# Exponentials among gelus and attention tiles over a batch's products: a re-planned gated-attention and spatial-gating kernel

## The chip, the cores and the metric

The kernel runs on one core of a Trainium2 chip. A core has five engines, each with its own instruction queue that is worked off in the order written: PE (matrix products), DVE and ACT (element-wise work, ACT also the functions that need a table: exp, log, gelu), POOL (element-wise work on data in on-chip memory) and SP, which here only issues DMA transfers. An instruction waits at the head of its queue until what it reads is there and what it overwrites has been read; everything behind it waits too. The metric is the device time of one execution in microseconds (us), as the median of several runs.

## The reference, cut

```python
# attention part: B, H, S, D = 4, 8, 768, 48
f = 1.0 / (1.0 + np.exp(-f_logit))
state = zeros((B, H, D, D))
for t in range(S):
    state = f[:, :, t, :, None] * state + einsum('bhd,bhe->bhde', k[:, :, t], v[:, :, t])
    y[:, :, t] = einsum('bhd,bhde->bhe', q[:, :, t], state)
x = y.transpose(0, 2, 1, 3).reshape(B, S, H * D)          # (4, 768, 384)

# gated MLP part: d_model 384, d_ff 1024
h = gelu_tanh(x @ w_in)
u, v = h[..., :512], h[..., 512:]
v_n = (v - mean(v)) / sqrt(var(v) + 1e-06) * g_ln          # over the 512 features
v_s = einsum('ts,bsd->btd', w_sg, v_n) + b_sg[None, :, None]
out = x + (u * v_s) @ w_out
```

The recurrence over time is a sum over earlier tokens with decaying weights, so the kernel computes it in chunks with matrix products.

## The kernel before

**Tiles.** Each of the 4 batches has 768 tokens, that is 6 tiles of 128, so 24 tiles, numbered n = 0 to 23. A tile's work is cut into *steps* with short names. The names are used below, so here they are, in the order in which a tile passes through them.

- Loads on SP: `f`, `k`, `q`, `v`.
- Gates: `e` and `l` (ACT: exp, then log, of the gate's logits), `lh`, `ll` (split into a high and a low part), `cum` (PE: cumulative sum), `up`, `dn` (ACT: exp of plus and of minus the sum), `mq`, `mk` (q and k times them).
- Turning q and k so that features lie on partitions. Tiles 0 to 5: `tr` (PE transposes) and `tc` (copies out). Tiles 6 to 23: `tt` (DVE transposes blocks of 32), `to` (DMA to the scratch tensor `kq_d`), `ti` (four DMAs back into the one tile `raw`), `tc` (two copies from `raw` into one of two `sk` tiles, on ACT or DVE). `ti` of tile n needs `tc` of tile n-1 to be done, since there is one `raw`.
- Attention: `su` (PE: 64 small products, scores and state updates, into `ps_s`), `ms` (DVE: mask), `sa`, `sm` (state), `y` (PE: 64 small products into `ps_y`), `ty`, `jy` (ACT copies, DVE adds the two halves of `ps_y`: the tile's x).
- MLP: `xT` (PE transposes x), `xh`, `xl` (ACT, DVE: high and low part), `hv` (PE: 9 products, 512 columns), `gv` (ACT: gelu), `ns`, `nd`, `nq`, `nr`, `nh`, `nl` (normalisation; `nd`, `nq`, `nh` on ACT). Per 3 tiles: `hu` (4 of 9 products) and `gu` (ACT: gelu). Per batch, once all six tiles are normalised: `sg` (8 of 18 products: the spatial product), `sb`, `sm_`, `sh`, `sl` (bias, gate, split), `po` (6 of 12 products), `re` (add x), `out` (store).
- Weights, once: `ld`, `wa` to `wf` (split into high and low parts on ACT, DVE, POOL) and `wT`, `wh`, `wl` (transposed `w_sg`).

**PSUM.** Four banks `ps_b` are shared by `cum`, `tr`, `xT`, `wT`, `hv`, `hu`, `sg` and `po`. A bank is held from the product to the last step that reads it: `hv` to its `gv`, `hu` to its `gu`, `cum` to its `dn`, `sg` to its `sb`, `po` to its `re`, `xT` to its `xl`. PE can't start a product while all four are held.

**What sets the order.** The class `Plan` decides, when the program is written, on which engine each step goes and in which order each engine's queue is written: a list scheduler with durations (`T`, and `W` for DMAs), due times, and a table `MOVES` that shifts due times and fixes engines for some steps. Nothing is decided on the chip. Due times come from a list `order` in which `merge` strews the next batch's attention steps between the products of the present batch, from share `A0` to share `A1` of them. Two costs matter here: `TABLE`, the time of a load of ACT's function table (exp and log are in one table, "E", gelu in another, "G"), and `HOLD`, which is added to the due time of an ACT step that would need the other table. On top of that, two lists of needs named `turn` forbid mixing: `e` of a batch needs the last `gu` and `gv` of the batch before, and each `gv` and `gu` of a batch needs all six `dn` of that batch. So each batch has one phase of exponentials and one of gelus.

**Fillers.** In the first 45 us of the plan, `warm` puts products of zeros (L1047) into stretches in which the plan has PE idle.

Of the kernel before, what the change touches and what calls it, by code (L numbers as in the profile page):

```python
# [63 lines left out]


MOVES = """
wfin0:-0.3:POOL wcin1:48.7 wdin1:106.3:DVE wein1:-89.2 wbin2:27.5 wqin2:32.3 wrin2:71.4 wdin2:34.7 wfin2:57.5:DVE
wbin3:31 wdin3:-0.5:POOL ldin4:0.2 wdin4:2.9:DVE ldin5:-428.9 ldin6:21.4 wdin6:0:DVE wfin6:30.8 wfin7:-35.2
ldout0:74.2 wfout0:0.5 ldout1:50.9 wcout1:144.3 ldout3:147 wrout3:87 wcout3:17.5 wfout3:22.1 wh1.0:-37.6 wT2.1:209.9
ldsg4:160.3 ldsg5:25.7 wh5.0:-25.3 wl5.0:1.4 v0:2.3 tc0.0:-149.1:DVE tc0.1:-170.6:ACT sa0.0:144.7 xh0:5.9 ns0:116.7  # L70
f1:-812.5 k1:-926.4 v1:3.6 mq1:-5:POOL do1:-14.2 tc1.1:-36.6:ACT sm1.1:-14.2:DVE hv1:545.1 v2:439.4 w2.0:-49.3:DVE
sm2.1:-68.3:DVE sg0.0:586.1 sh0.0:-74.9 sm_0.3:0:DVE mq3:7.6 mk3:-107.3 di3:-24.8 sm3.0:53.6:DVE sm3.1:0:POOL nq3:-6.3
nl3:-0.8 f4:28.7 q4:232.9 mq4:-143.4:POOL do4:158.4 di4:225.7:DVE su4:-20.1 sm4.0:26.5:POOL w5.0:344.2 w5.1:-181.4
mk5:-12.7:POOL di5:0.3:ACT gv5:17.2 sm_1.0:23 sl1.0:2.8 sm_1.1:56.2:DVE gu1.2:-28.9 hu1.3:30.8 sg1.3:701.8 sl1.3:-133
w6.0:0:POOL lh6:0:ACT ll6:-2.1 mq6:116.2:DVE tc6.1:112.2:ACT sm6.1:-39.6:DVE re6:-66.3 w7.0:330.6 ll7:-0.7:POOL
up7:73.8 mq7:199.7:DVE mk7:0:POOL sm7.0:25.9:POOL w8.0:-55.9 w8.1:104:POOL e8:24.5 lh8:-0.2 cum8:19.4 tc8.0:-24.4:DVE
su8:-8.5 sm8.0:0:POOL sa8.1:-29 xT8:80.9 sg2.0:205.7 sm_2.2:-53.8:POOL sm_2.3:0:DVE w9.1:-120.3 e9:241.9 ll9:0:POOL
mq9:0:POOL mk9:0:DVE tc9.0:-117:ACT y9:95.9 po9:929.6 w10.1:-30.3:DVE lh10:-23.6 ll10:19.8 ti10.3:0.9 tc10.0:263.6:ACT
w11.0:51.4:POOL lh11:5.2:ACT ll11:5.3:POOL mq11:-39:POOL tt11.0:-9.6 su11:-201.2 nr11:-106.6 sg3.0:1365 sg3.1:1534.6
sm_3.2:137.5 sg3.3:-186.9 re11:-108.1 mq12:0.3 mk12:-0.2:POOL lh13:-75.7 ll13:74.5 sm13.0:-110.3 nh13:-5.9  # L80
ll14:151.9:POOL tc14.0:-18.5:ACT su14:-305 sm_4.3:50.1 re14:8.3 ll15:190.5:DVE tc15.1:63.6:DVE sm15.1:129.3:DVE
xT15:-16.2 w16.0:-121.6 lh16:-156.5:ACT mk16:25.9:POOL tc16.1:162:DVE su16:-606.4 sm16.0:100.7 w17.1:0:POOL l17:-51.2
lh17:-306.2 mk17:-62.1:POOL sa17.0:12 sm17.0:1.6:DVE y17:-275.2 xT17:-1 hv17:-1.3 sg5.0:1216.7 sm_5.1:17.1:POOL
po17:1030.5 mk18:0:POOL tt18.0:28.5 ti18.0:83.3 ti18.3:185.4 tc18.1:69.4:DVE sz18:-10.6 w19.1:51.8:POOL e19:-85.2
ll19:-84.7:DVE ti19.2:-0.1 tc19.1:1.5 su19:-56.9 lh20:35.6 ll20:-89.1:DVE mq20:-3:DVE to20.0:-11.4 su20:-151.9
sb6.0:-93.1 sm_6.0:12.8 gu6.1:100.6 hu6.3:39.5 sg6.3:323.4 q21:6.2 lh21:10.2:ACT mk21:19.7:POOL q22:5.2 w22.1:144:POOL
ll22:-123.3:POOL mk22:-59.2:DVE to22.0:-0.5 tc22.0:16.9:ACT sm22.0:-160.4:POOL w23.0:114.5 w23.1:30.7:DVE
ll23:-67.8:POOL mk23:-30.6 di23.0:1.2 tc23.1:21.8:ACT sm23.0:135.1:DVE sm_7.0:35.3 sm_7.1:-62.3:DVE po23:-7.1
"""


# [1072 lines left out]
```

## Time and profile before

| | |
|---|---|
| median of 3 runs | 391.78 us (389.3 to 392.39) |
| the profiled execution's own time | 390.13 us |
| its span, first to last instruction | 388.3 us |
| mean granted TensorE clock | 0.983 |
| instructions | 11340 |
| DMA | 46.29 MB, mean 119 GB/s |

The span is 1.83 us shorter than the time of the same execution. In the profile, busy times are of one engine; "idle before" is the time an engine stood at the head of its queue before an instruction, and the name behind "<-" is the work that it waited for last. PEclk is the share of full speed that the matrix engine's clock was granted. The stages are read off by windows in us from the start of the span: the first products of `sg` begin at 80, the last batch's run to the end from 345. Rows of the written order, further down, carry the line numbers of the kernel that they belong to: behind the table `MOVES` the changed kernel's lines are three lower.

### The profile page before, as it was taken

The numbers are of one execution on the slowest core, as the hardware profiler recorded it, in microseconds if no ns is written. First come the engines' busy times: TensorE is split into PE (matmuls) and PEld (weight loads), VectorE is DVE, ScalarE is ACT, GpSimd is POOL, SyncE is SP. The second block draws the span as 40 slices with busy tenths as digits, with TensorE's granted clock in tenths as the row PEclk, the third lists the DMA queues.
The fourth block names the chain that finished last, engine by engine and source line by source line (L and its number), as shares of the span: only waits on it lengthen the run. The fifth ranks groups of instructions, "written<-read, shape, count | busy, mean of one in ns | idle before, by whom it ended". The sixth has DMA issues, their size and how long they took to land.

```text
span 388.3 us, 11340 instructions
## 1 busy us (share of the span) xinstructions
PE 364.0 (94%) x4672; PEld 330.1 (85%) x4672; DVE 247.7 (64%) x582; ACT 213.3 (55%) x482; POOL 53.5 (14%) x98
## 2 busy tenths in 40 slices
PE   8999999999997978999998799999989799999994
PEld 3677888899995958899988689999978698899994
DVE  5899889859857754339868654238748845335531
ACT  6576589894651546795462374847444475641100
POOL 2101422202121210104001111100212011100000
PEclk9999999999999999999999899999989899999998
DMA  9999995303668798102788984100577840000012
GB/s 177 228 244 192 216 257 139 100 2 95 152 141 190 170 202 144 22 0 64 186 190 187 190 172 83 22 20 23 125 195 185 171 126 3 22 1 2 1 47 81
DMA packets 145997, 46.29 MB, mean 119 GB/s; under 512 B 117524, under 2 KB 144532, under 8 KB 145940
## 3 DMA queue, kind: packets, MB, share of 16 engines
q1 hardware_dynamic: 145940, 45.51, 52.8%
q8 instruction: 38, 0.62, 0.7%
q14 instruction: 19, 0.16, 0.1%
HBM read 33.64 MB, written 11.85 MB: 117 GB/s over the span
## 4 chain that ended last, share of the span: by engine, by line
PE 48%; DMA 14%; DVE 13%; ACT 11%; SPq 6%; issue 6%; POOL 1%; ACTq 0%; DVEq 0%; POOLq 0%
PE ps_b L694 38%; DMA raw<-kq_d 8%; SPq L602 5%; PE ps_y L670 4%; ACT sk L328 3%; DMA kq_d<-f 2%; PE ps_s L622 2%; DVE kq L541 1%; PE ps_b L699 1%; ACT f L323 1%; DMA kq<-in_k_dram 1%; DMA vs<-in_v_dram 1%; ACT vg L323 1%; DVE st L632 1%; ACT vg L736 1%
## 5 line engine op out<-in xcount | busy, mean ns | idle before, releaser
L694 PE MATMUL ps_b<-w_sg_hi,vh 128*128 128x384 f32 x192 | 65.9, 343 | 0.0
L694 PE MATMUL ps_b<-w_sg_lo,vh 128*128 128x384 f32 x192 | 65.4, 341 | 0.0
L694 PE MATMUL ps_b<-w_sg_hi,vh_lo 128*128 128x384 f32 x192 | 65.4, 341 | 0.0
L694 PE MATMUL ps_b<-w_out_hi,gg 128*128 128x384 f32 x174 | 50.4, 354 | 0.0
L328 ACT COPY sk<-raw 112x512 f32<-112x512 f32 x32 | 18.8, 619 | 33.9 <-DMA raw<-kq_d 33.3
L694 PEld LDWEIGHTS ps_b<-w_sg_hi,vh 128*128 128x128 f32 x192 | 36.6, 191 | 0.1
L694 PEld LDWEIGHTS ps_b<-w_sg_lo,vh 128*128 128x128 f32 x192 | 36.6, 190 | 0.0
L694 PEld LDWEIGHTS ps_b<-w_sg_hi,vh_lo 128*128 128x128 f32 x192 | 36.5, 190 | 0.0
L781 DVE SCALAR_TENSOR_TENSOR tmp<-ps_b,cols,b_bc 128x384 f32<-128x384 f32 x32 | 19.5, 610 | 26.1 <-PE ps_b L694 26.0
L694 PEld LDWEIGHTS ps_b<-w_out_hi,gg 128*128 128x128 f32 x174 | 33.7, 199 | 0.3
L797 ACT CAST gg<-tmp 128x384 fp32r<-128x384 f32 x29 | 14.8, 512 | 34.6 <-DVE tmp L786 33.0
L622 PE MATMUL ps_s<-sk 48*64 48x64 f32 x768 | 23.8, 229 | 9.9 <-ACT sk L328 6.4
L622 PEld LDWEIGHTS ps_s<-sk 48*64 48x64 f32 x768 | 20.6, 133 | 13.5 <-ACT sk L328 10.2
L754 DVE SCALAR_TENSOR_TENSOR vh_lo<-vg,vg_rs,vh 128x512 fp32r<-128x512 f32 x24 | 18.0, 750 | 20.3 <-ACT vh L749 20.2
L694 PE MATMUL ps_b<-w_out_lo,gg 128*128 128x384 f32 x87 | 30.4, 349 | 0.0
L694 PE MATMUL ps_b<-xTh,w_in_hi 128*128 128x384 f32 x84 | 29.1, 346 | 0.0
L670 PEld LDWEIGHTS ps_y<-vs,st 64*64 64x64 f32 x768 | 24.7, 134 | 4.8 <-issue 3.2
L694 PE MATMUL ps_b<-xTh,w_in_lo 128*128 128x384 f32 x84 | 28.3, 337 | 0.3 <-issue 0.3
L694 PE MATMUL ps_b<-xTl,w_in_hi 128*128 128x384 f32 x84 | 28.4, 338 | 0.0
L323 ACT ACTIVATE f<-f 128x384 f32<-128x384 f32 x48 | 24.4, 520 | 6.8 <-DMA f<-in_f_logit_dram 6.3
L670 PE MATMUL ps_y<-vs,st 64*64 64x48 f32 x768 | 27.5, 220 | 0.3 <-ACT u L323 0.3
L694 PE MATMUL ps_b<-w_in_hi,xTl 128*128 128x512 f32 x63 | 25.1, 399 | 2.7 <-DVE xTl L719 2.7
(131 smaller groups left out, 874.3 us busy)
## 6 DMA issues: line engine op xcount, KB each, us to landing
f<-in_f_logit_dram SPq DMA_DIRECT2D x24, 192.0 KB, 3.7
kq<-in_k_dram SPq DMA_DIRECT2D x24, 192.0 KB, 3.7
kq<-in_q_dram SPq DMA_DIRECT2D x24, 192.0 KB, 4.4
vs<-in_v_dram SPq DMA_DIRECT2D x24, 192.0 KB, 3.2
raw<-kq_d SPq DMA_DIRECT2D x36, 128.0 KB, 2.6
out_dram<-tmp SPq DMA_DIRECT2D x24, 192.0 KB, 2.8
kq_d<-tmp SPq DMA_DIRECT2D x18, 192.0 KB, 2.3
kq_d<-f SPq DMA_DIRECT2D x18, 192.0 KB, 3.0
```

Of the source, the lines that this page charges most:

```text
L323: nc.scalar.activation(dst, src, func, **kw)
L328: (nc.scalar.copy if e == "ACT" else ENG[e].tensor_copy)(dst, src)
L541: ENG[e].tensor_mul(kt, kt, f_raw[n])
L602: ENG[e].dma_start(raw[row : row + r1 - r0].rearrange("d b a t -> d b (a t)"), kq_d[n, :, r0:r1, m].rearrange("b r j y -> r b (j y)"))
L622: nc.tensor.matmul(ps_s[rows(score_rows(c, 2 * p + par)), par, p * C : (p + 1) * C], sk[r, 0, p, c], sk[r, 1, p, c], start=True, stop=True)
L632: nc.vector.tensor_mul(sts[0], ps_s[:, :, 0 : NP * C].rearrange("s x (p t) -> s x p t", t=C), mask[:, None, None, :].to_broadcast((P, 2, N ...
L670: nc.tensor.matmul(ps_y[rows(c), half, h * D : (h + 1) * D], a, m, start=start, stop=stop)
L694: nc.tensor.matmul(ps, a, m, start=(j == 0), stop=(j == len(seq) - 1))
L699: nc.tensor.transpose(ps[:, j], x_sb[n][:, j * P : (j + 1) * P], ident)
L754: nc.vector.scalar_tensor_tensor(vl, v_raw.pop(n), rs, vh.bitcast(F32), op0=ALU.mult, op1=ALU.subtract)
L781: nc.vector.scalar_tensor_tensor(t, psum[f"sg{g}.{ft}"][:, :E], g_col[:, ft : ft + 1], b_bc[:, tokens(g)], op0=ALU.mult, op1=ALU.add)
L797: nc.scalar.copy(gt[(g, ft)][0], g_raw[(g, ft)])
```

## The change

It has four parts, none of which alters what is computed.

1. The two `turn` lists are emptied, so exponentials may stand among gelus, with a table load wherever the table changes. `HOLD` goes from 8 to 20.
2. `A0` and `A1` get a value for each batch; the attention tiles of the second batch are strewn over 0.25 to 0.85 of the first batch's products, those of the third and fourth over 0.05 to 0.75.
3. Some planned durations are changed: `tt` 0.65 to 0.48, the copies `tr_c` out of `raw` 0.467 to 0.49 on ACT and 0.6 to 0.46 on DVE, and the DMAs `to`, `ti` and `tj` (the short pieces) longer.
4. `MOVES` is another table, for the new plan.

```diff
-A0, A1 = 0.1, 0.8
+A0, A1 = (0.25, 0.05, 0.05), (0.85, 0.75, 0.75)
...
-    ok_e="DVE:0.25", ... tt="DVE:0.65", zr="POOL:2.2", tr_c="ACT:0.467 DVE:0.6", ...
+    ok_e="DVE:0.25", ... tt="DVE:0.48", zr="POOL:2.2", tr_c="ACT:0.49 DVE:0.46", ...
...
-W = dict(... to=(0.5, 0.65), ti=(0.4, 0.4), tj=(0.35, 0.25), out=(0.45, 0.58))
+W = dict(... to=(0.54, 0.9), ti=(0.43, 0.62), tj=(0.4, 0.45), out=(0.45, 0.58))
...
 MOVES = """
-wfin0:-0.3:POOL wcin1:48.7 wdin1:106.3:DVE wein1:-89.2 wbin2:27.5 wqin2:32.3 wrin2:71.4 wdin2:34.7 wfin2:57.5:DVE
...
+wbin0:388.1 wdin0:-42.7:POOL wcin1:371.6 wrin3:343.8 wcin3:-99.1 wdin3:305.4:DVE wdin4:86.5 wfin4:224.6:DVE wrin5:88.5
...
-    STAY, HOLD, SHIFT, AWAY = 194.7373, 8.0, 31.7708, 4.5365
+    STAY, HOLD, SHIFT, AWAY = 194.7373, 20, 31.7708, 4.5365
...
-            order += merge(units + rest, att, A0, A1)
+            order += merge(units + rest, att, A0[b - 1], A1[b - 1])
...
-        turn = [f"gu{2 * b - 1}.{NF - 1}", f"gv{n0 - 1}"] if (n0 := b * NT) else []
+        turn = [f"gu{2 * b - 1}.{NF - 1}", f"gv{n0 - 1}"] if (n0 := b * NT) < 0 else []
...
-        turn = [f"dn{n0 + j}" for j in range(NT)] if b else []
+        turn = []
         op(f"gv{n}", lambda e, n=n: gelu_v(n), T["gv"], [f"hv{n}"] + turn, table="G", take=("vg",), unbank=f"hv{n}")
```

**ACT, at the second batch's first gelus.** Before, the copies of an attention tile out of `raw` (L328) are followed by the only table load of this batch's gelu phase, and then gelus (`vg`) and normalisation alone:

```order
L797 CAST gg<-tmp 128x384
L328 COPY sk_97<-raw 112x512 x2
L321 ACT_TABLE_LOAD
L323 ACTIVATE vg,vg_mv<-ps_b_68 128x512
L736 ACTIVATE vg<-vg,vg_mv 128x512
L741 ACTIVATE vh_lo,vg_mv<-vg 128x512
```

Now, at the first gelus of the same batch (L320 is the line of table functions, `eb` and `f<-ps_b` are the exponentials `up` and `dn`):

```order
L320 ACTIVATE f,flag_e<-f 128x384
L320 ACTIVATE f<-f 128x384
L318 ACT_TABLE_LOAD
L320 ACTIVATE vg,vg_mv<-ps_b_70 128x512
L794 CAST gg<-tmp 128x384
L325 COPY sk_97<-raw 112x512 x2
L733 ACTIVATE vg<-vg,vg_mv 128x512
L318 ACT_TABLE_LOAD
L320 ACTIVATE eb_103<-ps_b_68 128x8x48
L794 CAST gg<-tmp 128x384
L320 ACTIVATE f<-ps_b_68 128x384
```

Between one gelu and the next a load, the exponentials of later tiles and a second load have moved in. In the whole program, without the branch for inputs out of range, there were 7 table loads after the first one and there are now 35.

**PE, at the third batch's first attention tile (tile 12).** Before, `su` of tile 12 (L622, L627) follows a spatial product of the batch before:

```order
L694 MATMUL ps_b_69<-w_sg_hi_80,vh 128x384
L694 MATMUL ps_b_69<-w_sg_lo_82,vh 128x384
L694 MATMUL ps_b_69<-w_sg_hi_80,vh_lo 128x384
L622 MATMUL ps_s<-sk_96 64x64 x4
L627 MATMUL ps_s<-vs_93,kq_90 48x48 x4
```

Now it follows `y` of tile 11 (L667), the last attention tile of the second batch, directly:

```order
L667 MATMUL ps_y<-S_101,sk_97 64x48 x2
L667 MATMUL ps_y<-vs_95,st 64x48
L667 MATMUL ps_y<-S_101,sk_97 64x48
L619 MATMUL ps_s<-sk_96 64x64 x4
L624 MATMUL ps_s<-vs_93,kq_90 48x48 x4
```

The third batch's attention has moved ahead of the second batch's spatial products; `su` of tiles 12 to 15 and `y` of tiles 12 to 14 now stand before or among the first of these, the rest after them. From `cum14` on, PE's steps there are now, by name: cum14, su11, y10, cum15, xT10, y11, su12, hv9. ACT's over the same stretch, from the last gelu ahead of it: a table load, up14, xh9, ty10, dn14, up15, dn15, xh10, and the two copies `tc` of tile 12. A little later PE has su14, hv12, sg2.0, cum16, y14, su15, and ACT, after the first copy of tile 14: xh12, gu3.2, nh11, ty13, a table load, e16, e18, l16, l18, lh16, e19, a table load, gv12, and the second copy of tile 15.

**PE, at the start.** Before, up to the first `su` (L524 is `cum`, L561 `do`, which picks the decays out, L576 `tr`):

```order
L1047 MATMUL ps_b_67<-zeros 128x512 x3
L524 MATMUL ps_b_67<-f,cs 128x384
L524 MATMUL ps_b_68<-f,cs 128x384
L1047 MATMUL ps_b_69<-zeros 128x512
L1047 MATMUL ps_b_67<-zeros 128x256
L561 MATMUL ps_b_69<-cs,eb_103 112x2 x4
L1047 MATMUL ps_b_67<-zeros 128x128
L576 MATMUL ps_b_70<-cs,kq_90 112x128 x4
L576 MATMUL ps_b_67<-cs,kq_90 112x128 x4
```

Now:

```order
L1044 MATMUL ps_b_67<-zeros 128x512 x2
L521 MATMUL ps_b_67<-f,cs 128x384
L1044 MATMUL ps_b_68<-zeros 128x512
L1044 MATMUL ps_b_68<-zeros 128x128
L521 MATMUL ps_b_68<-f,cs 128x384
L558 MATMUL ps_b_69<-cs,eb_102 112x2 x4
L573 MATMUL ps_b_70<-cs,kq_90 112x128 x4
L573 MATMUL ps_b_67<-cs,kq_90 112x128 x4
```

Over the whole start the fillers went from 21 instructions of together 8320 columns to 16 of 6656. From hv22 to the end (hv22, hv23, hu7, sg6, sg7, po18 to po23) PE's order is the same as before.

More of the change, by code (lines that the diff above doesn't have):

```diff
@@ L47 @@
     nl="DVE:0.663", gu="ACT:0.38", sb="DVE:0.534", sm_="DVE:0.468 POOL:1.05", sh="ACT:0.402", sl="DVE:0.467", re="DVE:0.467", ok="DVE:1.2",
-    ok_e="DVE:0.25", w="DVE:0.267 POOL:0.45", wT=0.25, cumf=0.72, cum=0.352, do=0.716, tr=0.791, tt="DVE:0.65", zr="POOL:2.2", tr_c="ACT:0.467 DVE:0.6", su=0.83, y=0.905, xT=0.25, hv=2.094, hu=1.584,
+    ok_e="DVE:0.25", w="DVE:0.267 POOL:0.45", wT=0.25, cumf=0.72, cum=0.352, do=0.716, tr=0.791, tt="DVE:0.48", zr="POOL:2.2", tr_c="ACT:0.49 DVE:0.46", su=0.83, y=0.905, xT=0.25, hv=2.094, hu=1.584,
     sg=3.167, po=2.084, ok_s=0.12,
 )
-W = dict(cs=(0.56, 0.5), g=(0.63, 0.1), b=(0.5, 2.1), ldin=(0.48, 1.26), ldout=(0.43, 1.12), ldsg=(0.42, 1.12), f=(0.46, 1.14), k=(0.43, 1.14), q=(0.6, 1.14), v=(0.45, 1.14), do=(0.58, 0.1), di=(0.42, 0.3), to=(0.5, 0.65), ti=(0.4, 0.4), tj=(0.35, 0.25), out=(0.45, 0.58))
+W = dict(cs=(0.56, 0.5), g=(0.63, 0.1), b=(0.5, 2.1), ldin=(0.48, 1.26), ldout=(0.43, 1.12), ldsg=(0.42, 1.12), f=(0.46, 1.14), k=(0.43, 1.14), q=(0.6, 1.14), v=(0.45, 1.14), do=(0.58, 0.1), di=(0.42, 0.3), to=(0.54, 0.9), ti=(0.43, 0.62), tj=(0.4, 0.45), out=(0.45, 0.58))
 RINGS = dict(f=4, lh=1, eb=2, u=8, gg=5, x=8, vg=2, vh=6, tmp=3)
@@ L66 @@
 MOVES = """
-wfin0:-0.3:POOL wcin1:48.7 wdin1:106.3:DVE wein1:-89.2 wbin2:27.5 wqin2:32.3 wrin2:71.4 wdin2:34.7 wfin2:57.5:DVE
[L68 to L86, printed above, removed]
@@ L87 @@
-ll22:-123.3:POOL mk22:-59.2:DVE to22.0:-0.5 tc22.0:16.9:ACT sm22.0:-160.4:POOL w23.0:114.5 w23.1:30.7:DVE
-ll23:-67.8:POOL mk23:-30.6 di23.0:1.2 tc23.1:21.8:ACT sm23.0:135.1:DVE sm_7.0:35.3 sm_7.1:-62.3:DVE po23:-7.1
+wbin0:388.1 wdin0:-42.7:POOL wcin1:371.6 wrin3:343.8 wcin3:-99.1 wdin3:305.4:DVE wdin4:86.5 wfin4:224.6:DVE wrin5:88.5
+wbin6:70.5 wfin6:-0.5:POOL wbin7:342.5 wrin7:222.5 wfin7:136.9:POOL ldout0:43.3 wfout0:-139 ldout1:444.3
+wdout1:136.6:POOL wfout2:61.6 waout3:53.5 wbout3:-15.3 wT0.0:91.5 wh0.1:-323.2 wh1.0:110.6 ldsg2:2 wT2.1:74.4
@@ new lines @@
+wT3.0:32.3 wT3.1:232.8 wh4.0:7.4 ldsg5:32.4 mk0:0:DVE gv0:144.9 sm1.0:199.8:DVE xl1:61.2 v2:144.4 mk2:12 sa2.0:-2.5
+sm2.0:340.9:DVE hu0.0:375.7 sm_0.0:-69.3:POOL sh0.0:-10.7 gu0.1:-79.4 sh0.1:-351.3 sm_0.2:73.7:DVE sg0.3:8.6
+sm_0.3:-17.5:POOL po2:3.4 q3:27.8 w3.0:279.8:POOL w3.1:134.8 mq3:18.2:POOL di3:0:ACT tr3:227.2 sa3.0:169.8
+sm3.0:-36.7:POOL xT3:264 w4.0:31.8:DVE sm4.0:0:POOL sm4.1:-12.4:POOL di5:-1.7:ACT sa5.0:15.5 nq5:-64.4 sg1.0:60.2
+hu1.1:-126.3 gu1.1:75.2 gu1.2:304 sg1.2:-16.5 sm_1.3:-21.7:POOL sh1.3:13.3 sl1.3:-78.5 w6.1:493.6 ll6:0:DVE
@@ new lines @@
+tt6.0:229.6 tc6.0:23:ACT jy6:-75.7 xh6:-10.7 hv6:871.9 w7.0:-989.6:DVE w7.1:12.5:DVE ll7:0:DVE up7:128.7 mq7:-20.5:DVE
+tt7.0:-318.4 re7:0.4 l8:57.9 cum8:383.5 mq8:-15.5:POOL mk8:-82.7:POOL ti8.3:80.5 tc8.1:6.9:DVE w9.0:0.2 mq9:70.4:POOL
+su9:-124.4 xh9:304.7 k10:3.4 w10.1:-0.7:POOL e10:94.9 ll10:0:POOL mq10:-57.5:POOL mk10:99.2:DVE ti10.0:58.9 y10:78.5
+k11:-124.5 lh11:66.2:ACT ll11:-2.8 mq11:2.7:POOL sg3.0:97.1 sg3.1:1.3 gu3.3:322.4 sg3.3:226.2 lh12:1.3:DVE up12:-79.1
+tc12.0:-7.4:ACT nh12:-0.2 nl12:70.3 w13.0:75.3 w13.1:15.3 lh13:-59.7:ACT tc13.0:-224.1:ACT tc13.1:28.3 sm13.0:132.2
@@ new lines @@
+nq13:46.6 v14:14.3 tc14.1:-0.4:DVE hu4.1:161 sm_4.1:0:POOL f15:1.4 lh15:97.8:DVE ll15:29:POOL mq15:26.2:DVE
+tc15.0:-201.2:DVE sm15.1:0.4:POOL f16:46.8 cum16:-214.9 ti16.2:-27.6 sm16.0:14 lh17:-144.9:DVE tc17.1:0:DVE sg5.1:84.7
+up18:-24.4 mq18:-24.2:POOL tt18.1:-11 tc18.0:2.9 hv18:176.5 ll19:44.9 mq19:61.5 mk19:63.2:POOL sm19.1:-76 ll20:3.7
+tc20.1:75.1:ACT hu6.1:185.8 sm_6.2:-119.2 sg6.3:95.4 sm_6.3:62.9 k21:-26.5 lh21:279.1:ACT tc21.0:-3.3 w22.0:-80.9
+w22.1:148.4:POOL lh22:0:DVE tc22.0:36:DVE tc22.1:0.9 sm22.0:-85.9:DVE sm22.1:200.1:DVE w23.1:24.1:POOL ll23:81.9:POOL
@@ L89 @@
+mk23:85.3 sm23.0:0:POOL
 """
```

## The prediction

> **What bounds the kernel now.** I read the busy times first, then stages, then what PE waits for, then the engines beside it.
>
> ```profile
> PE 364.0 (94%) x4672; PEld 330.1 (85%) x4672; DVE 247.7 (64%) x582; ACT 213.3 (55%) x482; POOL 53.5 (14%) x98
> ```
>
> PE is busy for 364.0 of 388.3 us and no other engine is near that. Neither the real matrix products nor their number changes, so only three things can pay: PE's idle time, fillers, and stretches at a reduced clock. The stages tell where these lie (span in us, length, then busy time of PE, PEld, DVE, ACT, POOL, the clock, the DMA share, GB/s):
>
> ```profile
> 0.00:80.00 80.00, 76.91 (x1078) 59.55 (x1079) 66.87 (x174) 57.72 (x132) 16.79 (x36) 1.00 0.88 188
> 80.00:345.00 265.00, 248.87 (x3379) 232.97 (x3378) 163.29 (x377) 150.97 (x342) 36.70 (x62) 0.98 0.51 113
> 345.00:388.00 43.00, 38.22 (x219) 37.61 (x217) 17.59 (x33) 4.60 (x9) 0.00 (x0) 0.97 0.08 30
> ```
>
> The last stage holds the same products in the same order after the change; I give it nothing. In the middle stage PE idles 265.00 - 248.87 = 16.1 us. Its waits there, by what ended them (us in total, times, longest):
>
> ```profile
> PE ps_s L622 <- ACT sk L328: 6.4, 5, 2.0
> PE ps_b L694 <- DVE xTl L719: 2.7, 1, 2.7
> PE ps_b L699 <- DVE x L678: 2.2, 1, 2.2
> PE ps_s L622 <- DVE S L648: 1.9, 3, 1.2
> PE ps_s L622 <- DVE sk L328: 1.6, 1, 1.6
> ```
>
> These five make 14.8 of the 16.1 us, and all belong to attention: L622 is su, waiting for the copies out of raw (8.0 us together) or for the state; the other two are hv and xT behind a fresh attention tile. No large wait is for a product in the banks. Behind the copies stands the turning of q and k. Two of its DMA issues and the copies that follow, in batch two:
>
> ```profile
> 132.40 3.10 SPq L602 DMA_DIRECT2D raw<-kq_d  x4
> 137.44 1.14 ACT L328 COPY sk<-raw 112x512 f32<-112x512 f32 x2 [4.17 <-DMA raw<-kq_d]
> 140.09 2.89 SPq L602 DMA_DIRECT2D raw<-kq_d  x4
> 145.89 1.14 ACT L328 COPY sk<-raw 112x512 f32<-112x512 f32 x2 [2.91 <-DMA raw<-kq_d]
> ```
>
> From copy to copy it takes 145.89 - 137.44 = 8.45 us. Where PE's queue puts tiles closer together than that for long, PE waits.
>
> The clock is a second cost of the same gaps. Two of three places, each a window of 3.4 us and the next (same columns as the stages):
>
> ```profile
> 214.50:217.90 3.40, 1.17 (x6) 0.64 (x5) 2.31 (x7) 1.60 (x3) 1.00 (x1) 1.00 0.65 123
> 217.90:221.30 3.40, 3.40 (x13) 3.40 (x14) 3.31 (x10) 0.48 (x1) 0.34 (x1) 0.51 1.11 224
> 303.20:306.60 3.40, 1.38 (x88) 1.20 (x79) 1.74 (x5) 2.24 (x4) 0.34 (x1) 1.00 1.23 194
> 306.60:310.00 3.40, 3.40 (x15) 3.40 (x12) 3.34 (x10) 1.61 (x4) 0.00 (x0) 0.51 0.76 169
> ```
>
> After a window in which PE worked for a third of the time, its clock is halved for one window, which costs about 3.4 x 0.49 = 1.7 us. Three such windows cost 5.1 us.
>
> **The change part by part.**
>
> *Table loads: 28 more.* The price is in the trace:
>
> ```profile
> L321 ACT ACT_TABLE_LOAD  x7: 1283/1283/1283, 39.4 to 305.9; - x7
> 125.98 1.14 ACT L328 COPY sk<-raw 112x512 f32<-112x512 f32 x2 [0.46 <-DMA raw<-kq_d]
> 127.14 1.28 ACT L321 ACT_TABLE_LOAD   x1
> 128.43 0.60 ACT L323 ACTIVATE vg<-ps_b 128x512 f32<-128x512 f32 x1
> ```
>
> The load begins 0.02 us after the copy ends (125.98 + 1.14) and gelu 0.01 us after the load, so a switch costs 1.28 us, with the usual overlap of neighbours lost, and 28 cost 35.9 us of ACT. By the built order 6 of the 35 stand before the middle stage (1 of 7 before), so the middle stage gets 23 more: 150.97 + 23 x 1.28 = 180.4 of 265 us, 68%. ACT stays below PE on average, and PE's four banks let it run ahead; that is the cover. If it fails, each load in front of a gelu or of dn keeps a bank and PE stands for up to 1.28 us. Behind a load queue all of ACT's steps, the copies of y and out of raw too, for which attention waits.
>
> The Trainium skill ("ScalarE: Activation LUTs", section "What ACT_TABLE_LOAD costs") gives about 1283 ns for the load plus 1380 ns of drain, 2.66 us a switch. The trace agrees on the load and shows no such drain. By the page the 28 loads would cost 74.5 us of ACT instead of 35.9.
>
> *Attention spread, gelus no longer held for the last dn.* This is to remove PE's 16.1 us. Its cost shows where the new order is tight. I take two such places and add both queues' rows. ACT's steps (middle stage, count, busy us, mean ns):
>
> ```profile
> L328 ACT COPY sk<-raw 112x512 f32<-112x512 f32 x32 | 18.8, 619 | 33.9 <-DMA raw<-kq_d 33.3 <-issue 0.5
> L323 ACT ACTIVATE f<-f 128x384 f32<-128x384 f32 x36 | 18.1, 518 | 4.8 <-DMA f<-in_f_logit_dram 4.6
> L749 ACT ACTIVATE vh<-vg,vg_rs 128x512 fp32r<-128x512 f32 x18 | 12.9, 719 | 4.9 <-POOL vg_rs L746 4.9
> L323 ACT ACTIVATE u<-ps_b 128x384 f32<-128x384 f32 x24 | 11.5, 485 | 5.4 <-PE ps_b L694 4.5 <-DVE w_out_lo L444 0.8
> L323 ACT ACTIVATE vg<-ps_b 128x512 f32<-128x512 f32 x18 | 10.7, 593 | 10.3 <-PE ps_b L694 9.8 <-DVE vh_lo L754 0.5
> L323 ACT ACTIVATE f<-ps_b 128x384 f32<-128x384 f32 x18 | 8.8, 489 | 0.0
> L323 ACT ACTIVATE eb<-ps_b 128x384 f32<-128x384 f32 x18 | 8.7, 485 | 7.6 <-PE ps_b L528 7.0 <-DMA dec_d<-eb 0.5
> L674 ACT COPY x<-ps_y 128x384 f32<-128x384 f32 x18 | 8.6, 475 | 9.8 <-PE ps_y L670 9.8
> L715 ACT CAST xTh<-ps_b 128x384 fp32r<-128x384 f32 x18 | 8.4, 474 | 7.8 <-PE ps_b L699 4.8 <-PE ps_b L694 2.9
> ```
>
> PE's: su (its 64 products), y, three transposes, and 126 products of 384 columns in a row, 22.25/126 = 0.177 us each, so cum 0.35, sg 3.18, and hv, whose nine have 512 columns, 9 x 0.177 x 512/384 = 2.1 (an estimate):
>
> ```profile
> 104.30:105.50 1.20, 1.09 (x64) 0.97 (x64) 0.00 (x0) 1.00 0.69 216
> 240.07 1.08 PE ps_y L670 x64
> 53.11 0.55 PE ps_b L699 x3
> 360.98 22.25 PE ps_b L694 x126
> ```
>
> Place one, cum14 to su12. ACT: 1.28 (load) + 2 x 0.485 (up) + 2 x 0.489 (dn) + 2 x 0.474 (xh) + 0.475 (ty10) + 1.14 (copies) = 5.8 us. PE up to su12: 2 x 0.35 + 1.09 + 2 x 1.08 + 0.55 = 4.5 us. PE waits 1.3 us. Place two, su14 to su15. ACT: 2 x 1.28 + 0.474 + 0.485 + 0.719 + 0.475 + 5 x 0.518 (e, l; lh put equal) + 0.518 + 0.593 + 0.619 = 9.0 us. PE: 1.09 + 2.1 + 3.18 + 0.35 + 1.08 = 7.8 us. PE waits 1.2 us. So 2.5 us come anew at the two tightest places. Elsewhere tiles lie further apart: from su15 to su16 four whole sg and more, where 8.45 us are covered. I leave a third of the old 16.1 us there, 5.4, because raw, its DMAs and SP's order of them remain. In all 7.9 us of waits are left: **-8.2**. Ends: all 16.1 gone, or the old 16.1 plus 2.5.
>
> *Clock.* With waits halved and no longer in clumps, I let two of three windows go: **-3.4** (ends -5.1 and 0).
>
> *Fillers.*
>
> ```profile
> 0.00:45.00 45.00, 19.24 (x42) 7.88 (x42) 1.00 1.08 214
> ```
>
> This row is the fillers' alone: 42 records, 19.24 us. The built program has 8320 columns of them before and 6656 after, so 19.24 x 1664/8320 = 3.85 us of PE work fall away. But the DMA share there is 1.08, and a filler not written may leave a wait for data in its place. Half: **-1.9** (ends 0 and -3.85). The start's ACT gets 5 more loads, 6.4 us on 57.72 of 80; DVE, 66.87 of 80, covers that, being busier still.
>
> *Switching between small and full products* happens 62 instead of 58 times in PE's steps. The nearest row is PE's own issue before y:
>
> ```profile
> PEld ps_y L670 <- issue: 2.2, 10, 0.3
> ```
>
> 0.22 us each, so 4 x 0.22: **+0.9** (ends 0 and +0.9).
>
> *The new step times* are plan figures and cost nothing on the chip. The new MOVES change engines for some copies, products and splits on DVE, ACT and POOL: the same work at 64%, 55% and 14% busy, hidden under PE. The DMAs are the same ones; on SP's queue ti of tile 10 now stands behind two loads and that of tile 9 behind fewer stores. I price that at nothing: it is in the 5.4 us left.
>
> Sum: 390.13 - 8.2 - 3.4 - 1.9 + 0.9 = 377.5 us, against the profiled execution's own time, which lies 1.65 us under the median of 391.78.
>
> **The rivals.**
>
> *Table loads on the path (slower).* Place: middle stage, PE held because the four banks wait for gelus or dn behind loads, as at the two places above. Each exposed load costs up to 1.28 us. The savings of 12.6 us are used up by 10 exposed loads of the 28 beyond those counted, and 14 of them give 377.5 + 14 x 1.28 = 395 us. For it: nearly every gelu group now has a load at each end, and ACT at 68% is not far from full in the attention stretches. Against: in the rows of before, ACT idles 33.9 us ahead of the copies alone, and PE never waits long for a bank. Chance 0.12. The skill's page above, section "Table sets: the hidden batching unit", speaks for this rival: activations should be batched by table set, which is what the kernel did and no longer does; here the trace does not settle it.
>
> *The waits only move (same).* The 8.45 us loop through raw stays, and tiles still come in twos and threes (su11, su12; su13, su14, su15). If 16.1 us of waits and all three slow windows remain, only fillers and switches count: 390.13 - 1.9 + 0.9 = 389.1. For it: PE's waits were almost all at attention tiles, and there are as many as before. Against: between them now lie products that used to stand together. Chance 0.18.
>
> *Everything goes.* All waits, slow windows and fillers: 390.13 - 16.1 - 5.1 - 3.85 = 365.1 us. The 2.5 us found above speak against it. Chance 0.05.
>
> **How the numbers follow.** Forecast 377.5, chance 0.65; its own range is 370 to 386. Runs of this kernel spread by 3 us, so about 1% of 391.78, up to 387.9 or 395.7, can't be told from no change. Faster: 0.65 + 0.05 = 0.70. Same: 0.18. Slower: 0.12. The range for 8 in 10 takes in the forecast's and the rival at 389.1, and leaves out the slow rival and the best case: 369 to 391.
>
> **What would show it.** In the new profile PE's idle time between the first sg and the last batch should be near 8 us, with copies from raw releasing under 4; the granted clock above 0.983; ACT_TABLE_LOAD 35 times at 1.28 us, ACT near 249 us in all; fillers near 15.4 us. Waits of PE for gelus or exponentials, or of ACT's copies behind loads, beyond 12 us in all would make the prediction wrong, as would as many half-speed windows as before, or a first sg that begins no earlier than 80 us.

## The result and the profile after

| | before | after |
|---|---|---|
| median of 4 runs | 391.25 us (389.3 to 392.39) | 380.38 us (379.31 to 382.39) |
| the profiled execution's own time | 390.13 us | 379.31 us |
| its span | 388.3 us | 377.5 us |
| mean granted clock | 0.983 | 0.992 |

The ratio is 0.9733, with a 95% interval of 0.9676 to 0.9791: the changed kernel is faster. The forecast was 377.5 us in a range of 369 to 391. Ratios leave out runs that are over 1.5% above the fastest of their kernel; medians are over all runs.

The busy times of the kernel after:

```profile
PE 359.7 (95%) x4662; PEld 324.7 (86%) x4662; DVE 250.7 (66%) x588; ACT 244.7 (65%) x507; POOL 51.9 (14%) x95
```

ACT works 31.4 us more than before and PE is busier by share, over a shorter span. The stages, with the cuts at the first spatial product (77.6, it was near 80) and at the last batch's (333.2, it was near 345); the columns are those of the table of stages before:

```profile
0.00:77.60 77.60, 72.83 (x1114) 56.76 (x1114) 62.69 (x162) 63.96 (x143) 17.10 (x36) 1.00 0.96 204
77.60:333.20 255.60, 248.48 (x3339) 230.22 (x3333) 169.22 (x389) 176.16 (x356) 34.84 (x59) 0.99 0.50 114
333.20:377.50 44.30, 38.37 (x219) 37.76 (x217) 18.80 (x39) 4.60 (x9) 0.00 (x0) 0.97 0.08 29
```

In the middle stage PE idles 255.60 - 248.48 = 7.1 us where it idled 16.1. Its waits there, by what ended them:

```profile
PE ps_b L696 <- DVE x L675: 2.4, 3, 0.9
PE ps_s L619 <- ACT sk L325: 1.6, 2, 1.1
PE ps_b L696 <- ACT vg L320: 0.9, 1, 0.9
PE ps_b L525 <- POOL ll L512: 0.6, 1, 0.6
PE ps_b L450 <- DVE w_sg_lo L939: 0.6, 1, 0.6
```

The old list began with 6.4 us of `su` behind the copies out of `raw`; that is now 1.6. The waits behind a gelu (`vg`, 0.9) are new and small. In the start, PE's two longest waits are new too, and its idle time rises there:

```profile
PE ps_b L691 <- ACT vg L320: 1.3, 1, 1.3
PE ps_y L667 <- issue: 1.2, 1, 1.2
```

ACT's groups in the middle stage:

```profile
L318 ACT ACT_TABLE_LOAD x30 | 38.5, 1283 | 0.5
L325 ACT COPY sk<-raw 112x512 f32<-112x512 f32 x29 | 17.4, 617 | 5.4 <-DMA raw<-kq_d 5.1 <-issue 0.3
```

Thirty table loads take 38.5 us of ACT, at 1283 ns each. The number to look at is the idle time ahead of the copies: 33.9 us before, 5.4 now. ACT used to stand at the head of its queue until `raw` had landed. The loads have moved into a part of that time: in experiment 1, which has none of them, it is 13.8 us, so some 8 of the 28.5 us that went were taken by loads and some 20 by other work.

The place that the prediction called place one, on PE and, in the last row, on ACT:

```profile
151.77 0.44 PE L525 MATMUL ps_b<-ll,cum 128*128 128x384 f32 x1 [0.64 <-POOL ll L512]
153.10 0.55 PE L696 MATMUL ps_b<-cs,x 128*128 128x128 f32 x3 [0.89 <-DVE x L675]
155.82 0.34 PE L619 MATMUL ps_s<-sk 48*64 48x64 f32 x8 [1.10 <-ACT sk L325]
...
154.63 1.14 ACT L325 COPY sk<-raw 112x512 f32<-112x512 f32 x2 [0.47 <-DMA raw<-kq_d]
```

Three waits, 0.64 + 0.89 + 1.10 = 2.6 us within 5 us, more than a third of all that is left in the stage. The window with them and the next one:

```profile
152.70:156.10 3.40, 1.90 (x87) 1.61 (x88) 1.37 (x4) 2.85 (x7) 0.00 (x0) 1.00 0.78 168
156.10:159.50 3.40, 3.40 (x67) 2.92 (x58) 2.01 (x5) 0.05 (x1) 0.00 (x0) 0.51 0.82 139
```

PE works 1.90 of 3.40 us and its clock is halved in the following window. It is the only such window left before the last batch's end; there were three.

### The profile page after: what moved, and what is told of

The parts are those of the page before. It is cut to its first block, busy times and chain, and to the rows that moved or that the text cites. A ratio compares the mean times of both kernels' runs of the same rounds, so it can differ in the third digit from the quotient of the medians.

```text
span 377.5 us, 11316 instructions
## 1 busy us (share of the span) xinstructions
PE 359.7 (95%) x4662; PEld 324.7 (86%) x4662; DVE 250.7 (66%) x588; ACT 244.7 (65%) x507; POOL 51.9 (14%) x95
## 4 chain that ended last, share of the span: by engine, by line
PE 55%; ACT 18%; DMA 10%; DVE 8%; SPq 3%; issue 3%; POOL 1%; ACTq 0%
PE ps_b L691 40%; ACT L318 5%; PE ps_b L1044 4%; PE ps_y L667 3%; DMA raw<-kq_d 3%; ACT vg L320 2%; ACT sk L325 2%; SPq L599 2%; DMA f<-in_f_logit_dram 2%; ACT f L320 2%; ACT vg L733 2%; ACT vh L746 2%; PE ps_s L619 2%; PE ps_b L521 1%; DMA kq<-in_q_dram 1%
## 5 line engine op out<-in xcount | busy, mean ns | idle before, releaser
L691 PE MATMUL ps_b<-w_sg_hi,vh 128*128 128x384 f32 x192 | 65.7, 342 | 0.0
L691 PE MATMUL ps_b<-w_sg_lo,vh 128*128 128x384 f32 x192 | 64.8, 338 | 0.0
L691 PE MATMUL ps_b<-w_sg_hi,vh_lo 128*128 128x384 f32 x192 | 64.8, 338 | 0.0
L691 PE MATMUL ps_b<-w_out_hi,gg 128*128 128x384 f32 x174 | 48.1, 339 | 0.4 <-ACT f L320 0.4
L318 ACT ACT_TABLE_LOAD x35 | 44.9, 1283 | 0.6
L794 ACT CAST gg<-tmp 128x384 fp32r<-128x384 f32 x29 | 14.8, 511 | 43.8 <-DVE tmp L783 37.7
L691 PEld LDWEIGHTS ps_b<-w_sg_hi,vh 128*128 128x128 f32 x192 | 36.0, 188 | 0.6 <-DVE w_sg_lo L939 0.2
L691 PEld LDWEIGHTS ps_b<-w_sg_lo,vh 128*128 128x128 f32 x192 | 36.1, 188 | 0.1
L691 PEld LDWEIGHTS ps_b<-w_sg_hi,vh_lo 128*128 128x128 f32 x192 | 36.0, 188 | 0.0
L320 ACT ACTIVATE f<-f 128x384 f32<-128x384 f32 x48 | 24.6, 522 | 12.9 <-DMA f<-in_f_logit_dram 12.6
L691 PEld LDWEIGHTS ps_b<-w_out_hi,gg 128*128 128x128 f32 x174 | 31.7, 188 | 1.0 <-ACT f L320 0.8
L691 PE MATMUL ps_b<-xTh,w_in_hi 128*128 128x384 f32 x84 | 29.3, 348 | 1.8 <-ACT vg L320 1.7
L667 PEld LDWEIGHTS ps_y<-vs,st 64*64 64x64 f32 x768 | 24.7, 134 | 6.5 <-issue 5.2
L691 PE MATMUL ps_b<-w_out_lo,gg 128*128 128x384 f32 x87 | 29.1, 335 | 0.0
L667 PE MATMUL ps_y<-S,sk 48*64 48x48 f32 x768 | 27.4, 220 | 1.2 <-issue 1.2
L691 PE MATMUL ps_b<-xTl,w_in_hi 128*128 128x384 f32 x84 | 28.4, 338 | 0.0
L691 PE MATMUL ps_b<-xTh,w_in_lo 128*128 128x384 f32 x84 | 28.4, 338 | 0.0
L691 PE MATMUL ps_b<-w_in_hi,xTh 128*128 128x512 f32 x63 | 26.9, 427 | 0.9 <-DVE xTl L716 0.9
L667 PE MATMUL ps_y<-vs,st 64*64 64x48 f32 x768 | 27.7, 220 | 0.0
```

The costliest lines, as they stand in the source:

```text
L318: nc.scalar.preload_act_table_set(SETS[want])
L320: nc.scalar.activation(dst, src, func, **kw)
L667: nc.tensor.matmul(ps_y[rows(c), half, h * D : (h + 1) * D], a, m, start=start, stop=stop)
L691: nc.tensor.matmul(ps, a, m, start=(j == 0), stop=(j == len(seq) - 1))
L794: nc.scalar.copy(gt[(g, ft)][0], g_raw[(g, ft)])
```

## The experiments

All ratios below are against the kernel before, timed on the same chip in the same session. "The table" is `MOVES`. Experiments on the changed kernel start from it unless another is named.

**1. No loads.** The gelus are replaced by exponentials, so that ACT never changes its function table. The written order stays as it is; the values after the gelus are other ones.

```diff
-        act(v_raw[n], psum[f"hv{n}"], AF.Gelu_apprx_tanh, accum_out=v_st[n][0][:, 0:1])
+        act(v_raw[n], psum[f"hv{n}"], AF.Exp, accum_out=v_st[n][0][:, 0:1])
...
-        act(uT[(g, ft)], psum[f"hu{g}.{ft}"][:, :E], AF.Gelu_apprx_tanh)
+        act(uT[(g, ft)], psum[f"hu{g}.{ft}"][:, :E], AF.Exp)
```

> The changed kernel with each gelu replaced by an exponential of the same size, so that no table is loaded after the first one; every other instruction and its place stay. The outputs are then not the reference's. Theory (loads are hidden behind PE but for a few tight places such as cum14 to su12): 376 to 379 us against 380.4, at most 4 us of the 44.9 us of loads come back. Rival (loads lie on the path in many places): 372 us or less, 8 us or more come back.

Measured: 376.59 us (375.63 to 377.45), ratio 0.9604 [0.9521, 0.9686]. The busy times, and the one load that is left in the program:

```profile
PE 360.6 (96%) x4662; PEld 327.5 (87%) x4662; DVE 249.0 (66%) x588; ACT 201.5 (54%) x472; POOL 52.7 (14%) x95
...
L300 ACT ACT_TABLE_LOAD x1 | 1.3, 1283 | 0.7 <-PEq L1144 0.7
```

ACT loses 43.2 us of work and the kernel 380.38 - 376.59 = 3.8 us (by the ratios about 5). Thirty-five loads therefore cost between 0.1 and 0.15 us each, about a tenth of their duration; the rest lies beside PE. The intervals of the two ratios overlap, so this is a size and not an exact price. PE's waits for a gelu, in the whole kernel after 1.7 us at L691 and 0.9 at L696, are gone without the loads. The copies out of `raw`, for comparison with 33.9 and 5.4 us above:

```profile
L325 ACT COPY sk<-raw 112x512 f32<-112x512 f32 x31 | 18.6, 618 | 13.8 <-DMA raw<-kq_d 12.7 <-DMA dec<-dec_d 1.1
```

**2. Loads twice.** Each load is issued a second time.

```diff
             nc.scalar.preload_act_table_set(SETS[want])
+            nc.scalar.preload_act_table_set(SETS[want])
```

> The changed kernel with every table load issued twice: 35 more loads of 1.28 us, 44.9 us more of ACT, nothing else. Theory (mostly hidden): 383 to 392 us, that is 0.1 to 0.25 of what is added. Rival (on the path in many places): 400 us or more. If ACT has no slack left at all: 425 us.

Measured: 381.66 us (380.5 to 383.28), ratio 0.9749 [0.9664, 0.9834]. Before that is read as "35 more loads cost nothing", the row of the loads:

```profile
L318 ACT ACT_TABLE_LOAD x35 | 44.9, 1283 | 0.6
```

There are 35, as without the edit, and ACT's busy time is 244.7 us as before it. The program has 11316 instructions, as without the edit, so the second loads were not executed. Whether the chip skipped them or the program lost them on its way there is not shown. This run repeats the changed kernel (at 381.66 against 380.38 us), and the expectation on dearer loads stays untested.

**3. Mixing undone, table kept.** Both `turn` lists are put back; the spread, the step times and the table stay.

```diff
-        turn = [f"gu{2 * b - 1}.{NF - 1}", f"gv{n0 - 1}"] if (n0 := b * NT) < 0 else []
+        turn = [f"gu{2 * b - 1}.{NF - 1}", f"gv{n0 - 1}"] if (n0 := b * NT) else []
...
-        turn = []
+        turn = [f"dn{n0 + j}" for j in range(NT)] if b else []
```

> The changed kernel with both lists of needs put back, so exponentials and gelus are in phases again (9 loads); spread, step times and MOVES stay those of the change, though MOVES was made for the other order. Theory (the mixing is what lets the attention tiles come early and apart): 387 us or more, PE idle in the middle back over 12 us. Rival (the gain comes from the spread, the new step times and MOVES alone): 379 to 383 us.

Measured: 403.67 us (403.12 to 407.87), ratio 1.0328 [1.0225, 1.0432], slower than before. Its loads, its copies (between 80 and 360 us of the span) and PE's first wait:

```profile
L318 ACT ACT_TABLE_LOAD x9 | 11.5, 1283 | 0.1
...
L325 ACT COPY sk<-raw 112x512 f32<-112x512 f32 x31 | 18.2, 618 | 27.4 <-DMA raw<-kq_d 27.4
...
PE ps_b L696 <- DVE x L675: 11.8, 9, 2.5
```

With 9 loads instead of 35 the idle time ahead of the copies is back (27.4 us), and PE waits 11.8 us to transpose x of tiles whose attention has just ended.

**4. Spread undone, table kept.**

```diff
-A0, A1 = (0.25, 0.05, 0.05), (0.85, 0.75, 0.75)
+A0, A1 = (0.1, 0.1, 0.1), (0.8, 0.8, 0.8)
```

> The changed kernel with A0, A1 = 0.1, 0.8 for all batches as before; MOVES was made for the other spread. Theory (spread matters beside the mixing): 383 to 388 us, with waits of su for the copies out of raw over 4 us. Rival (spread matters little once mixing is allowed): 379 to 382 us.

Measured: 394.45 us (392.27 to 397.74, 10 runs), ratio 1.0083 [1.0032, 1.0134], above the range expected. PE's waits of `su` for the copies out of `raw` are 2.8 us and not over 4; the largest sum, 4.8 us, is for x of tiles whose attention has just ended. What 3 and 4 can't tell is whether the part or its table is at fault: the table's shifts were made for the other due times. Hence the next five, all without a table.

**5 to 9. The parts without a table.** In each, `MOVES` is empty, and in the last three one part is undone besides: the `turn` lists as in 3, the spread as in 4, or the step times of before.

```diff
 MOVES = """
-wbin0:388.1 wdin0:-42.7:POOL wcin1:371.6 ...
-...
 """
...
-tt="DVE:0.48", tr_c="ACT:0.49 DVE:0.46", ... to=(0.54, 0.9), ti=(0.43, 0.62), tj=(0.4, 0.45)
+tt="DVE:0.65", tr_c="ACT:0.467 DVE:0.6", ... to=(0.5, 0.65), ti=(0.4, 0.4), tj=(0.35, 0.25)
```

Before without its table:

> The kernel before with an empty MOVES: the planner's own order, without hand-set or searched shifts. Both theories: slower than 392, since the table was made for it; 400 to 415 us. It is the base for the next three.

After without its table:

> The changed kernel with an empty MOVES. Theory (the rules themselves, mixing and spread, bring the gain; MOVES brings each version about as much): 10 us or more below the kernel before without MOVES. Rival (the table of shifts brings the gain, found anew for the change): within 4 us of the kernel before without MOVES.

The same without mixing:

> The changed kernel with an empty MOVES and both lists of needs put back: phases of exponentials and gelus, new spread and step times. Theory (mixing is needed for the spread to work): 8 us or more above the changed kernel without MOVES. Rival (phases cost nothing by themselves, the 403.7 us with MOVES came from a table made for another order): within 4 us of it.

The same with the old spread:

> The changed kernel with an empty MOVES and A0, A1 = 0.1, 0.8 throughout: mixing, new step times, old spread. Theory (spread is worth something beside mixing): 4 us or more above the changed kernel without MOVES. Rival (the 394.5 us with MOVES came from a table made for another spread): within 3 us of it.

The same with the old step times:

> The changed kernel with an empty MOVES and the planned durations (T and W) of the kernel before; mixing, spread and HOLD stay new. Theory (the durations matter, since the plan promised the turning of q and k too early): 3 to 8 us above the changed kernel without MOVES, 403 to 408 us. Rival (durations so near each other hardly change an order): 399 to 402 us.

| no table | us | ratio to before with its table | loads after the first |
|---|---|---|---|
| 5. before | 419.57 | 1.0763 [1.0675, 1.085] | 15 |
| 6. after | 400.35 | 1.024 [1.0151, 1.0329] | 37 |
| 7. after, phases kept apart | 409.1 | 1.0469 [1.0363, 1.0576] | 11 |
| 8. after, old spread | 405.66 | 1.0401 [1.0325, 1.0477] | 47 |
| 9. after, old step times | 410.83 | 1.0513 [1.0448, 1.0578] | 35 |

Without tables the change is worth 419.57 - 400.35 = 19.2 us. Undoing one part costs 8.7 us (mixing), 5.3 (spread; its interval touches that of 6) or 10.5 (step times). Experiment 9 was timed in another session than 5 to 8; by the ratios it costs 10.7. 5 and 9 came out slower than expected. The three add to 24.5, more than the whole, which suggests that the parts overlap, but the intervals are too wide to show it. The change of `HOLD` was not undone in any run. The table is worth 419.57 - 390.73 = 28.8 us to the kernel before (390.73 is its median in that session) and 400.35 - 380.38 = 20.0 to the kernel after: read as one sum, a table made for the old rules had already taken back about 9 us of what these rules cost, and 19.2 us of better rules showed as 10.9. How far each of the two tables could still be improved was not tested.

**10 and 11. No fillers**, in the kernel after and in the kernel before.

```diff
-    steps = plan.warm(plan.run(), 45.0, ...
+    steps = plan.warm(plan.run(), 0.0, ...
```

> The changed kernel without its 16 fillers (14.8 us of PE work in the start). Theory as in the prediction (half of a filler is on the path): 373 us. Rival one (PE would wait for data there in any case): 379 to 381 us. Rival two (without fillers the clock drops to half in the start): 382 us or more, with half-speed windows before 45 us.

> The kernel before without its 21 fillers (19.2 us of PE work). Theory (half on the path): 381 us. Rival one (all hidden): 389 to 391 us. Rival two (clock drops in the start): 393 us or more.

Measured: after 386.49 us (384.01 to 387.51, 6 runs), ratio 0.9851 [0.9801, 0.9902], so 6.1 us more than with its fillers by the medians and 4.6 by the ratios; before 394.26 us (391.84 to 400.28, 12 runs), ratio 1.0072 [1.0037, 1.0107], so about 3 us more. A gain was forecast for both. The first 45 us of the kernel after, of the fillers in it alone, and then of experiment 10:

```profile
0.00:45.00 45.00, 42.73 (x676) 30.51 (x677) 35.08 (x92) 31.68 (x74) 8.56 (x19) 1.00 1.02 208
0.00:45.00 45.00, 14.79 (x32) 6.16 (x32) 1.00 1.02 208
```

```profile
0.00:45.00 45.00, 36.23 (x562) 29.00 (x563) 31.31 (x83) 27.97 (x67) 7.18 (x18) 1.00 1.06 212
```

With fillers PE spends 42.73 - 14.79 = 27.9 us on 644 records that are not fillers; without them 36.2 us on only 562. The same products take longer. The first cumulative sums of the gates in the kernel after, and then in experiment 10 (ns: shortest, median, longest):

```profile
L521 PE MATMUL ps_b<-f,cs x12: 486/528/1009, 4.8 to 37.4; 128*128 128x384 f32 x12
```

```profile
L521 PE MATMUL ps_b<-f,cs x12: 486/847/1009, 4.8 to 40.0; 128*128 128x384 f32 x12
```

The clock column says 1.00 for these 45 us in both, but its records begin only at 6.0 us in the kernel after and at 31.8 in experiment 10; the durations show that PE runs slowly before. In experiment 10 that lasts until 31.8 us, and two more slow stretches follow, the second in place of the one window that the kernel after has at 156 us (same columns as the stages):

```profile
55.70:62.50 6.80, 6.69 (x65) 6.46 (x66) 4.84 (x14) 5.25 (x12) 0.00 (x0) 0.50 0.77 177
161.50:168.40 6.90, 5.26 (x72) 4.49 (x73) 4.46 (x12) 2.21 (x6) 0.00 (x0) 0.51 1.01 187
```

The fillers pay by keeping the clock up, not by filling time.

**12. Planned anew.** The same steps with another written order, and other engines for 116 steps. Some planned durations are changed once more (not in this cut).

```diff
-    TABLE = 1.28
+    TABLE = 1.42
...
-            s["due"] += float(us)
-            if e:
-                s["engines"] = {e[0]: s["engines"][e[0]]}
+            s["due"], s["engines"] = float(us), {e: s["engines"][e]}
...
-    STAY, HOLD, SHIFT, AWAY = 194.7373, 20, 31.7708, 4.5365
+    STAY, HOLD, SHIFT, AWAY = 0.0, 0.0, 31.7708, 4.5365
```

> The changed kernel with the same steps and needs, but another written order and other engines for 116 steps: due time and engine of every step now come from a table of their own, made by a new search with step times corrected by this case's traces (a table switch 1.42 us instead of 1.28, copies out of raw 0.515 on ACT and 0.49 on DVE, the DMA pieces back into raw 0.15 longer); the costs for switching tables and product kinds are left to the search. It keeps about as many table loads (33) and fillers (6272 columns instead of 6656). Under the same corrected times the changed kernel's own order ends at 371.3 in the plan and took a span of 377.5 on the chip; this one ends at 363.9. Theory (what is left in the changed kernel is order, not work: the rest of PE's named waits and of the fetch stalls can be planned away where the step times are right): span 370 to 373, time 372 to 375, PE idle in the middle stage under 5 us. Rival (the search fits the plan's errors; the last 7 us that the plan doesn't see move elsewhere): time 378 or more, as many waits of PE as in the changed kernel, at other places.

Measured: 377.98 us (375.01 to 379.43, 6 runs), ratio 0.9662 [0.9614, 0.9711]. Its middle stage and PE's longest waits in it (a table row for every step has pushed the lines down by 240):

```profile
78.40:331.00 252.60, 247.84 (x3332) 229.12 (x3329) 168.94 (x371) 166.26 (x338) 65.91 (x99) 1.00 0.53 115
```

```profile
PE ps_b L931 <- DVE gg L1038: 1.0, 1, 1.0
PE ps_b L764 <- DVE tmp L1049: 1.0, 1, 1.0
PE ps_s L859 <- ACT sk L565: 0.9, 1, 0.9
```

PE's idle time there falls to 4.8 us, as expected, and no half-speed window is left before the end. Yet the span fell by 2.5 us and not by the 4.5 to 7.5 expected: some waits went, and two of 1.0 us came where there were none, at `po` behind a gate's split and at a `cum` behind the bank of a residual. The median is 2.4 us below the changed kernel's, but the intervals of the two ratios overlap, so it is not shown to be faster than that; it has the lowest median of the versions run here that compute the reference.

## Why the prediction came out right, and where its steps did not

- **The waits** were the main term: -8.2 forecast, 16.1 - 7.1 = 9.0 us measured. Place one was undersized (1.3 forecast, 2.6 found), because only ACT's queue was summed against PE's: one of the three waits there was for POOL's `ll` and one for DVE's x. Place two was oversized (1.2 against one wait of 0.5). Elsewhere 5.4 were allowed and 7.1 - 2.6 - 0.5 = 4.0 are left. Copies out of `raw` release 1.6 us there, under the 4 named.
- **The clock**: in the two profiled executions two of three half-speed windows went, as forecast, and the one left follows place one. That this is a gain of the change is not shown: the profiled execution of before, at 0.983, has a low clock. The 48 runs of the kernel before in the later sessions, on three chips, lie between 0.980 and 0.998, with a median of 0.988, and the four of the kernel after at 0.992, 0.987, 0.989 and 0.987. So the -3.4 was hit with luck.
- **Table loads**: 35 at 1.283 us, ACT at 244.7 us against about 249. The rival that they lie on the path falls: experiment 1 takes them all away and gains 3.8 us. The Trainium skill ("ScalarE: Activation LUTs", section "What ACT_TABLE_LOAD costs") has a drain beside the load that would double the switch; the row in the prediction, with the gelu 0.01 us after the load, is not contradicted by any run here. Its rule to batch activations by table set (section "Table sets: the hidden batching unit") would have kept the phases; here experiments 3 and 7, which keep them, are slower with a quarter to a third of the loads, 9 and 11.
- **Fillers**: the step that failed. Forecast was -1.9, half of 3.85, on the view that fillers are partly work in the way. Their row did fall, from 19.24 to 14.79 us, but experiment 10 shows that they are not simply a cost to be saved: without any, the kernel is 4.6 to 6.1 us slower, because the clock stays low. No run takes out just the fifth that the change dropped. Nor is the shorter start (77.6 us to the first `sg`, 80.2 before) a gain of that size: idle time in it rose (77.60 - 72.83 = 4.8 us, about 3.1 before), and work left it. PE's transposes of `w_sg` in the kernel after, in the start and in the middle stage (this line's PE and PEld time):

```profile
0.00:77.60 77.60, 2.81 (x18) 2.21 (x18) 1.00 0.96 204
77.60:333.20 255.60, 2.67 (x18) 2.07 (x18) 0.99 0.50 114
```

  Before, 33 of them stood in the start and 3 behind it. One group of `hu` (9 products) moved the same way, and one `su` and two `cum` the other way. So a first `sg` that begins earlier, which the prediction took as a sign, shows only that the order changed.
- **Switching** was +0.9. PE's weight loads ahead of `y` with no releaser but "issue":

```profile
PEld ps_y L667 <- issue: 5.2, 17, 1.3
```

  In the whole run of before there were 13 such gaps, together 3.2 us. The four more were forecast. Three of them are in the middle stage, 13 against 10, and cost 3.2 - 2.2 = 1.0 us, close to the price forecast. The other 1.0 us is in the start, where one gap is far longer than the rest:

```profile
34.24 0.14 PEld L667 LDWEIGHTS ps_y<-vs,st 64*64 64x64 f32 x2 [1.31 <-issue]
```

  PE's own row at `y` has 1.2 us of it as idle time. Why this gap is long was not found out.
- **The last batch** was given nothing and its stage is 0.8 us longer, 44.3 us against 43.5 with the cut of before at its first product. Up to the last residual the two agree within 0.1 us; the difference lies behind it, in the last store, and no reason was found.
- **The step times** were costed at nothing on the chip. For the sum that was harmless, since it was made from the order as written. As a statement about the change it hid a large part: experiment 9 puts them at 10.5 us without the table, and mixing at 8.7, with intervals that overlap.

The whole account, from PE's records taken from start to start, fillers apart: idle -7.3 us over the whole run, fillers -3.8, half-speed windows -3.4 (10.2 us of products fell into them before and 3.5 now; half of the difference), the end +0.8. These make -13.7 of a measured -10.8, so 2.9 us came back in PE's other products. The dearer switches can be at most 0.8 of them (2.0 less the 1.2 that is idle time already); the rest was not followed. The forecast was -12.6. Idle time is -9.0 in the middle stage and +1.7 in the start; with the fillers' -3.8 that makes -2.1 for the start, near the -1.9 forecast, although work also left it and the reasoning failed. So the forecast's terms came out near their sizes, two of them (clock and fillers) by luck, and what it put at little or nothing, other products, switches and the end, took 1.8 us off the gain.

## What to carry to other kernels

Before grouping work to save a fixed cost on one engine, look at what that engine waits for: here ACT stood 33.9 us ahead of its copies and worked 55% of the span, all 35 loads of 1.28 us cost about 4 to 5 us, and without a table the grouping cost 8.7. When a searched table sits on a planner, judge a change of the planner's rules both without a table and with one made for it; the new table under partly old rules (experiments 3 and 4) was slower than either kernel. Give the planner durations near those of the trace: it is a change of the order, and here a part as large as mixing. In the trace of before, transposes of `tt` in a row begin 0.495 us apart (planned 0.65, then 0.48) and copies out of `raw` on ACT 0.52 us apart (0.467, then 0.49).

## What the runs showed of the hardware that was not expected

- A busy PE was not enough to bring the clock up early on. In experiment 10 PE worked without a break from 14.8 to 18.2 us (columns of the stages), and the eight products of a `tr` at 20.36 us still took nearly twice as long as at 8.71 us in the kernel after, where 3.8 us of long products of zeros had run before 6 us (last row). Which property of the work decides is not shown:

```profile
14.80:18.20 3.40, 3.40 (x72) 3.25 (x72) 3.37 (x10) 0.00 (x0) 0.00 (x0) 1.00 1.40 188
20.36 1.91 PE L573 MATMUL ps_b<-cs,kq 128*112 128x128 f32 x8
...
8.71 1.06 PE L573 MATMUL ps_b<-cs,kq 128*112 128x128 f32 x8
```

- Where a gap lies matters as well as how long it is. The half-speed windows of before begin at 217.95, 286.22 and 306.70 us, which are 20 and 6 times 3.41 us apart. In windows laid on these steps, half speed followed 1.18, 1.83 and 1.39 us of work, and in the kernel after 1.94. The longest wait of before (2.7 us, up to 123.82) falls across two such windows, and full speed stayed:

```profile
118.97:122.38 3.41, 2.17 (x110) 1.68 (x100) 1.29 (x4) 0.48 (x1) 0.00 (x0) 1.00 1.19 213
122.38:125.79 3.41, 1.97 (x9) 1.66 (x10) 3.05 (x8) 0.52 (x1) 1.22 (x1) 1.00 0.81 239
136.03:139.45 3.42, 1.71 (x63) 1.43 (x65) 0.97 (x4) 1.78 (x5) 0.00 (x0) 1.00 0.82 164
282.81:286.22 3.41, 1.83 (x69) 1.48 (x68) 2.49 (x5) 2.06 (x5) 0.99 (x1) 1.00 0.75 203
```

  The third row, with less work than the last, was followed by full speed too, so PE's busy time alone doesn't decide, and "a third of the time" in the prediction fits two of the three windows.
- In experiment 12 the spread between runs goes with the granted clock: the six runs had spans of 373.2, 374.2 and 375.0 us at 0.997, 0.995 and 0.996, and 377.3, 377.5 and 377.6 at 0.987, 0.991 and 0.987. In the kernel before the tie is loose: one run took 391.48 us at 0.995, one 387.58 at 0.989.
- A second load of the same table, issued right behind the first, does not appear in the trace (experiment 2: 35 loads, as without it); what dropped it is not shown.
